# Modulation columns in 1 KB-run half loads, four feature blocks of K in one run, and an earlier load of reciprocal rows, in a transformer-block kernel

## The chip, the cores and the metric

The kernel runs on one core of one Trainium2 chip. The metric is device time in microseconds (us) of that core, from repeated executions; "span" is the same execution as the hardware profiler sees it, about 1.8 us shorter. The granted TensorE clock is given with each run as the mean over its span; 1.0 is full speed.

## The reference

One block of a diffusion transformer: layer norm with modulation, linear attention, and a gated feed-forward, for 2048 tokens of width 1024. The change touches the modulation and the K projection of the first part (cut to what matters):

```python
mod = (_silu(c) @ w_mod).reshape(c.shape[0], 6, 1, -1)
sa, ca, ga, sb, cb, gb = ...                    # shift, scale, gate of either part
h = _layernorm(x, axis=-1) * (1 + ca) + sa      # (2048, 1024)
q, k, v = split(h @ wqkv)                       # 32 heads of 32
pq, pk = phi(q), phi(k)                         # phi(t) = where(t > 0, t + 1, exp(t)) + 1e-6
# ... attention, x = x + ga * o @ wo, then the feed-forward with sb, cb, gb
```

K of any token therefore needs the shift and scale columns of w_mod (2 x 1024 x 1024, 4 MB) as well as wk (2 MB) and x, and all of that comes through one DMA queue.

## The kernel before

K is computed as h (transposed, features on partitions) times wk, in eight feature blocks of 128 that are summed in PSUM. Two feature blocks are a "quarter". For each quarter, TensorE makes the shift (t=0) and scale (t=1) of its 256 features as 32 matmuls with one column each, VectorE copies them out of PSUM and scales two blocks of h with them, and TensorE can run these two blocks of K. "Warming" matmuls of zeros keep TensorE in use while nothing else is there for it. The loads, in the order of the queue:

```python
x_dma(0, 1); x_dma(1, 2)                 # 256 KB a chunk of 128 tokens
wmq_dma(0, (1,))                         # w_mod, one quarter's scale: 512 KB in 512 B runs
x_dma(2, 3)
wmq_dma(0, (0,))                         # the same quarter's shift
w_dma(WK, OFF_WK, "wk", 1, 0, D, 0, 2)   # wk feature blocks 0 and 1, 512 KB in 2 KB runs
x_dma(3, 4)
for q in range(1, 4):
    wmq_dma(q)                           # 2 x 512 KB
    for d0, d1 in ((2 * q, 2 * q + 1), (2 * q + 1, 2 * q + 2)):
        w_dma(WK, OFF_WK, "wk", 1, 0, D, d0, d1)   # 256 KB each
# ... wq, more x
```

The opening as each engine's order has it (cut: the part for quarters 2 and 3 follows in the same manner):

```python
t1(0, 5); ln1_bn(1, 1); ln1_fin(1)       # t1: eight transposes of a chunk; ln1_*: layer norm
warm(6, 7)                               # six warming matmuls
mod_cols(0, 4)                           # 32 one-column matmuls of quarter 0
ln1_bn(2, 0); xhat_dve(1, *xh_buf(1)); t1(1, 6); ln1_bn(2, 1); ln1_fin(2)
mod_copy(0, 4); mod1(0, 1, 0, 2)         # VectorE: copy out, scale blocks 0-1 of chunk 0
warm(3, 7)
k_part(0, [0])                           # K, blocks 0-1, tokens 0-127
# ... k_part(0, [1]), k_part(0, [2]), mod_cols(1, ...), ...
```

The other place is 220 us later, ahead of the feed-forward: `rb_load(3, (0,))`, a broadcast load of reciprocal rows for the attention's denominator, stands behind three DMA transposes in the same queue.

## Time and profile before

| what | before |
|---|---|
| time, three first runs | 834.2 us (833.83 to 834.79) |
| span, mean clock | 832.2 us, 1.0 |
| first K matmul starts | 10.85 us |
| first Q matmul starts | 30.69 us |
| feed-forward starts | 234.42 us |
| wait for the up weights at 252 us | 0.59 us |

The profile is that of one execution. The views used are the page (shares of busy time, the span in 40 slices), the timeline of an engine (start, duration, instructions in a row, and in brackets the idle time before them and who ended it), and the table by stretches (busy time of each engine in each stretch, with the granted clock). A load's landing is the start of its DMA issue plus the time from issue to landing that the tile view gives. How to read them is shown in the prediction below, with the lines themselves.

Matmuls overlap, so durations do not show the rate; starts do. At full clock 512-column matmuls start 0.216 us apart, at half the clock 0.427 us.

### The profile page before, as it was taken

What the parts mean: (1) busy time and instruction counts of PE and PEld (TensorE: products, weight loads), DVE (VectorE), ACT (ScalarE), POOL (GpSimd) and SP (SyncE); (2) the same over time, 40 slices, a digit from 0 to 9 for tenths busy, and PEclk for the clock granted to TensorE, in tenths of its full rate; (3) what the DMA queues carried; (4) which work ended last, traced back from release to release, by engine and by line L of the source; (5) the groups of instructions that cost most, each with busy time, mean ns of one, the idle gap of its engine ahead of it and who ended that gap; (6) DMA issues with size and microseconds to landing.
All of it is one profiled execution on the core that took longest, in us unless ns stands there. A gap on an engine that the chain in (4) does not pass through costs nothing.

```text
span 832.2 us, 11518 instructions
## 1 busy us (share of the span) xinstructions
PE 821.7 (99%) x4179; PEld 391.9 (47%) x4253; DVE 509.7 (61%) x920; ACT 321.3 (39%) x542; POOL 36.2 (4%) x90
## 2 busy tenths in 40 slices
PE   8999999999999999999999999999999999999998
PEld 4444446665444444444444444444444444444445
DVE  6799888834776577753555565355556535555522
ACT  2597642323523354410444441044444104444300
POOL 2122200000200000000000000000000000000000
PEclk9999999999999999999999999999999999999999
DMA  9788769358999789170555533065553306555000
GB/s 288 230 182 223 166 136 274 48 121 195 205 254 289 227 244 262 31 173 19 158 153 152 151 102 76 20 163 152 154 146 102 76 20 171 155 152 137 7 20 26
DMA packets 216929, 121.90 MB, mean 146 GB/s; under 512 B 69276, under 2 KB 206756, under 8 KB 215848
## 3 DMA queue, kind: packets, MB, share of 16 engines
q1 hardware_dynamic: 216856, 121.16, 56.1%
q8 instruction: 34, 0.56, 0.3%
q14 instruction: 23, 0.19, 0.1%
q10 hardware_dynamic: 16, 0.00, 0.0%
HBM read 103.03 MB, written 4.47 MB: 129 GB/s over the span
## 4 chain that ended last, share of the span: by engine, by line
PE 92%; SPq 3%; DMA 3%; issue 1%; DVE 1%; ACT 0%; ACTq 0%
PE ps_all L1359 23%; PE ps_all L1334 22%; PE ps_all L1331 21%; PE ps_all L826 7%; PE ps_all L862 7%; PE ps_all L811 5%; PE ps_all L1193 5%; DMA wu<-in_B_w_up_dram 2%; SPq L568 1%; DMA wmq<-in_w_mod_dram 1%; SPq L1172 1%; SPq L573 1%; PE ps_all L844 0%; PE ps_all L1121 0%; SPq L562 0%
## 5 line engine op out<-in xcount | busy, mean ns | idle before, releaser
L1334 PE MATMUL ps_all<-h2T,wu 128*128 128x512 bf16 x896 | 339.6, 379 | 2.3 <-DMA wu<-in_B_w_up_dram 0.4
L1331 PE MATMUL ps_all<-h2T,wg 128*128 128x512 bf16 x860 | 325.9, 379 | 0.0
L1359 PE MATMUL ps_all<-wd,yT 128*128 128x512 bf16 (+3 forms) x934 | 193.1, 366 | 0.9
L1342 ACT ACTIVATE q<-ps_all 128x512 f32<-128x512 f32 x112 | 66.9, 597 | 222.3 <-PE ps_all L1331 217.1
L1359 PEld LDWEIGHTS ps_all<-wd,yT 128*128 128x128 bf16 x952 | 90.1, 98 | 103.7 <-issue 0.2
L1334 PEld LDWEIGHTS ps_all<-h2T,wu 128*128 128x128 bf16 x896 | 87.7, 98 | 106.5 <-DMA wu<-in_B_w_up_dram 0.9
L1331 PEld LDWEIGHTS ps_all<-h2T,wg 128*128 128x128 bf16 x896 | 87.7, 98 | 105.6
L1347 DVE SCALAR_TENSOR_TENSOR ww<-th,guh 128x512 f32<-128x512 f32 x112 | 77.5, 692 | 77.9 <-ACT th L1346 77.9
L1344 DVE SCALAR_TENSOR_TENSOR ww<-q,ps_all 128x512 f32<-128x512 f32 x112 | 76.9, 687 | 74.5 <-ACT guh L1343 74.3
L1346 ACT ACTIVATE th<-ww 128x512 f32<-128x512 f32 x112 | 70.5, 629 | 87.5 <-DVE ww L1344 87.5
L1364 DVE TENSOR_TENSOR ps_all<-ps_all,gbb 128x512 f32<-128x512 f32 (+3 forms) x34 | 22.7, 667 | 94.6 <-PE ps_all L1359 94.6
L1349 DVE TENSOR_TENSOR yT<-ww,ps_all 128x512 bf16<-128x512 f32 x112 | 76.9, 686 | 3.8
L1343 ACT ACTIVATE guh<-ps_all 128x512 f32<-128x512 f32 x112 | 66.3, 592 | 0.0
L862 PE MATMUL ps_all<-h1T,wq 128*128 128x512 bf16 x256 | 56.7, 379 | 0.0
L1193 PE MATMUL ps_all<-w,pq 128*128 128x512 bf16 x252 | 56.3, 379 | 0.2
L811 PE MATMUL ps_all<-wk,h1T 128*128 128x512 bf16 x239 | 55.3, 379 | 1.2 <-DMA wk<-in_A_wqkv_dram 0.5
L800 ACT ACTIVATE eb<-ps_all 128x512 f32<-128x512 f32 x64 | 36.4, 593 | 38.1 <-PE ps_all L811 14.8
L862 PEld LDWEIGHTS ps_all<-h1T,wq 128*128 128x128 bf16 x256 | 25.0, 98 | 29.9
L1193 PEld LDWEIGHTS ps_all<-w,pq 128*128 128x128 bf16 x256 | 24.9, 98 | 30.0 <-ACT w L1123 0.3
L811 PEld LDWEIGHTS ps_all<-wk,h1T 128*128 128x128 bf16 x248 | 23.6, 97 | 28.9 <-DVE h1T L691 2.3
L826 PE MATMUL ps_all<-xall,pk 128*128 128x342 bf16 (+1 forms) x216 | 35.2, 307 | 0.0
L630 ACT ACTIVATE xhd<-xall,nm,rs 128x1024 bf16<-128x1024 bf16 x12 | 14.9, 1240 | 38.2 <-DVE nm L620 31.7
(97 smaller groups left out, 506.6 us busy)
## 6 DMA issues: line engine op xcount, KB each, us to landing
wg<-in_B_w_gate_dram SPq DMA_DIRECT2D x56, 512.0 KB, 3.9
wu<-in_B_w_up_dram SPq DMA_DIRECT2D x56, 512.0 KB, 5.2
rb<-scr_rd SPq DMA_DIRECT2D x32, 256.0 KB, 5.8
wd<-in_B_w_down_dram SPq DMA_DIRECT2D x7, 1024.0 KB, 8.9
wmst<-in_w_mod_dram SPq DMA_DIRECT2D x6, 1024.0 KB, 6.4
wmq<-in_w_mod_dram SPq DMA_DIRECT2D x8, 512.0 KB, 7.5
out_dram<-xall SPq DMA_DIRECT2D x31, 128.0 KB, 1.7
xall<-in_A_x_dram SPq DMA_DIRECT2D x3, 1024.0 KB, 9.1
```

The costliest lines, as they stand in the source:

```text
L811: o = sch.op(T, lambda e, dc=dc: e.matmul(PS(bank), H1[sg][:, ci, dc, :], W_[:, dc, jg * 512:(jg + 1) * 512], start=(dc == 0), stop=(dc == ...
L826: o = sch.op(T, lambda e, c_=c_: e.matmul(PS(bank, 0, n), PK[c_][:, g * P:(g + 1) * P], xrow(c_, o_, o_ + n), start=(c_ == 0), stop=(c_ == ...
L862: o = sch.op(T, lambda e, dc=dc: e.matmul(PS(b), WQ[:, dc, qc * P:(qc + 1) * P], H1[sg][:, :, dc, :], start=(dc == 0), stop=(dc == NDC - 1 ...
L1193: last[half] = sch.op(T, lambda e, g=g, half=half: e.matmul(PS(b0 + half), PQ[sg][:, g, ci * P:(ci + 1) * P], W2[:, g, half * 512:(half + ...
L1331: og = sch.op(T, lambda e, dc=dc: e.matmul(PS(bg), WG[slot][:, dc, e_ * P:(e_ + 1) * P], H2[sg][:, dc, :], start=(dc == 0), stop=(dc == ND ...
L1334: ou = sch.op(T, lambda e, dc=dc: e.matmul(PS(bu), WU[slot][:, dc, e_ * P:(e_ + 1) * P], H2[sg][:, dc, :], start=(dc == 0), stop=(dc == ND ...
L1342: sch.op(A, lambda e: e.activation(Q1[j][:, :], PS(bg), ACTF.Square, scale=math.sqrt(GELU_A)), prd=pr(bg), wr=rq, note=f"q1 {fc}")
L1344: sch.op(V, lambda e: e.scalar_tensor_tensor(WW[j][:, :], Q1[j][:, :], 1.0, PS(bg), op0=ALU.add, op1=ALU.mult), rd=rq, prd=pr(bg), wr=rw, ...
L1346: sch.op(A, lambda e: e.activation(TH[j][:, :], WW[j][:, :], ACTF.Tanh, scale=GELU_C), rd=rw, wr=rt, note=f"th {fc}")
L1347: sch.op(V, lambda e: e.scalar_tensor_tensor(WW[j][:, :], TH[j][:, :], 1.0, GUH[j][:, :], op0=ALU.add, op1=ALU.mult), rd=rt + rg, wr=rw, n ...
L1349: sch.op(V, lambda e: e.tensor_tensor(YT[:, fc, :], WW[j][:, :], PS(bu), ALU.mult), rd=rw, prd=pr(bu), wr=r_yt(fc), note=f"yT {fc}")
L1359: o = sch.op(T, lambda e, b=b, fc=fc, c0=c0, c1=c1, n=n: e.matmul(PS(b, 0, n), YT[:, fc, ci * P:(ci + 1) * P], WDT[fc // 4][:, fc % 4, c0:c1],
```

## The change

The intent: longer runs (1 KB for 512 B) for the first half of the shift and scale columns, so that they load faster; both halves ahead of wk, so that K of tokens 0 to 383 can go through four feature blocks without a stop for the next quarter; and the reciprocal rows earlier, so that the up weights behind them are not late. The core of the diff (cut marked):

```diff
+        def wmh_dma(t):
+            sch.dma(Q, lambda e: e.dma_start(WMST[1 - t][:], wm_v[:, :, t * D:t * D + 512]), wr=r_wm(1 - t), note=f"wmh{t}")
+
         x_dma(0, 1)
         x_dma(1, 2)
-        wmq_dma(0, (1,))
+        wmh_dma(1)
         x_dma(2, 3)
-        wmq_dma(0, (0,))
+        wmh_dma(0)
         w_dma(WK, OFF_WK, "wk", 1, 0, D, 0, 2)
         x_dma(3, 4)
-        for q in range(1, 4):
+        for d0 in (2, 3):
+            w_dma(WK, OFF_WK, "wk", 1, 0, D, d0, d0 + 1)
+        for q in range(2, 4):
             wmq_dma(q)
 ...
-        warm(6, 7)
-        mod_cols(0, 4)
+        warm(3, 7)
+        mod_cols(0, 4, (1,))
+        mod_cols(1, 4, (1,))
         ln1_bn(2, 0)
         xhat_dve(1, *xh_buf(1))
         t1(1, 6)
         ln1_bn(2, 1)
         ln1_fin(2)
+        xhat_dve(2, *xh_buf(2))
+        mod_cols(0, 4, (0,))
+        t1(2, 7)
         mod_copy(0, 4)
         mod1(0, 1, 0, 2)
-        warm(3, 7)
+        mod1(1, 1, 0, 2)
         k_part(0, [0])
 ... (K of blocks 0 to 3 for tokens 0-383, then the last chunk, then quarters 2 and 3)
             if c_ == 4:
                 pq_scale(1, 1, GH[0] + GH[1])
+                rb_load(3, (0,))
             wo_chunk(c_, 2 * (c_ % 4))
 ...
-            if c_ == 6:
-                rb_load(3, (0,))
```

One half (512 of 1024 features of scale, or of shift) is now one load of 1 MB in 1 KB runs.

More of the change, by code (lines that the diff above doesn't have):

```diff
@@ L723, in mod_cols @@
             rng = [(bank * 2048 + (MC0 + q * 4) * 4, bank * 2048 + (MC0 + q * 4 + 4) * 4)]
+            rq0 = [(bank * 2048 + MC0 * 4, bank * 2048 + (MC0 + 4) * 4)]
             for t in ts:
@@ L726, in mod_cols @@
                     col = MC0 + q * 4 + t * 2 + b
+                    c0 = q * 256 + b * P
                     for dc in range(NDC):
-                        o = sch.op(T, lambda e, t=t, b=b, dc=dc, col=col: e.matmul(
-                            PS(bank, col, col + 1), WMQ[q][:, dc, t, b * P:(b + 1) * P], SILUT[:, dc:dc + 1],
+                        ap = WMST[1 - t][:, dc, c0:c0 + P] if q < 2 else WMQ[q][:, dc, t, b * P:(b + 1) * P]
+                        o = sch.op(T, lambda e, ap=ap, dc=dc, col=col, t=t, b=b: e.matmul(
+                            PS(bank, col, col + 1), ap, SILUT[:, dc:dc + 1],
                             start=(q == b == dc == 0 and t == 1), stop=(dc == NDC - 1), skip_group_check=True),
-                            rd=r_wmq(q, t) + r_sm("siluT"), pwr=(rng if dc == 0 else ()), note=f"mod{q}.{t}.{b}.{dc}")
+                            rd=(r_wm(1 - t, dc, dc + 1) if q < 2 else r_wmq(q, t)) + r_sm("siluT"), pwr=((rng + (rq0 if (q, t) == (1, 0) else [])) if dc == 0 else ()), note=f"mod{q}.{t}.{b}.{dc}")
             for t_ in rng:
@@ L933, in bass_adaLN_cond__linear_attn_block__geglu_ffn__prompt_kernel @@
         ln1_fin(2)
+        xhat_dve(2, *xh_buf(2))
+        mod_cols(0, 4, (0,))
+        t1(2, 7)
         mod_copy(0, 4)
         mod1(0, 1, 0, 2)
-        warm(3, 7)
+        mod1(1, 1, 0, 2)
         k_part(0, [0])
-        xhat_dve(2, *xh_buf(2))
-        t1(2, 7)
-        mod1(1, 1, 0, 2)
+        mod_cols(1, 4, (0,))
         ln1_bn(3, 0)
         ln1_bn(3, 1)
+        mod1(2, 1, 0, 2)
+        mod_copy(1, 4)
+        k_part(0, [1])
+        k_part(0, [2])
         ln1_fin(3)
-        k_part(0, [1])
-        mod1(2, 1, 0, 2)
-        mod_cols(1, 4, (0,))
-        k_part(0, [2])
+        mod1(0, 2, 2, 4)
+        k_tiles([2, 3], [(0, 0), (0, 1)])
+        k_tiles([2], [(1, 0), (1, 1)])
         xhat_dve(3, *xh_buf(3))
-        mod_cols(1, 4, (1,))
-        mod_copy(1, 4)
+        mod1(2, 1, 2, 4)
         t1(3, 7)
-        mod1(0, 3, 2, 4)
-        k_tiles([2, 3], [(0, 0), (0, 1), (1, 0), (1, 1)])
-        k_tiles([2], [(2, 0), (2, 1)])
+        k_tiles([3], [(1, 0), (1, 1)])
+        k_tiles([2, 3], [(2, 0), (2, 1)])
         mod1(3, 1, 0, 4)
+        mod_cols(2, 4, (0,))
         k_part(0, [3])
         k31([2, 3])
-        mod_cols(2, 4, (0,))
-        k_tiles([3], [(2, 0)])
         mod_cols(2, 4, (1,))
         mod_copy(2, 4)
-        k_tiles([3], [(2, 1)])
         k_tiles([2, 3], [(3, 0)])
```

## The prediction

> **What bounds the kernel now.** I read the page's shares of busy time first, then the TensorE timeline with the idle time before each group, then the DMA view of the opening and the timeline of the DMA-issuing queue around the one late wait.
>
> ```profile
> span 832.2 us, 11518 instructions
> PE 821.7 (99%) x4179; PEld 391.9 (47%) x4253; DVE 509.7 (61%) x920; ACT 321.3 (39%) x542; POOL 36.2 (4%) x90
> ```
>
> TensorE is busy for 821.7 of 832.2 us, so only some 10 us are left that are not matmul time, about 2 us of them the launch and 2.5 us the last store. Nothing in this change touches the bulk of the matmuls. The question is where TensorE waits, and the timeline of TensorE tells (start, duration, instructions, idle time before them and who ended it):
>
> ```profile
> 8.70 1.19 PE L728 MATMUL ps_all<-siluT,wmq 128*128 128x1 bf16 x32
> ...
> 10.85 1.03 PE L811 MATMUL ps_all<-wk,h1T 128*128 128x512 bf16 x4
> ...
> 16.49 2.32 PE L811 MATMUL ps_all<-wk,h1T 128*128 128x512 bf16 x10 [0.46 <-DMA wk<-in_A_wqkv_dram]
> ...
> 21.01 0.55 PE L728 MATMUL ps_all<-siluT,wmq 128*128 128x1 bf16 x16 [0.53 <-DMA wmq<-in_w_mod_dram]
> ...
> 27.27 2.97 PE L811 MATMUL ps_all<-wk,h1T 128*128 128x512 bf16 x13 [0.23 <-DVE h1T L691]
> 30.07 0.77 PE L897 MATMUL ps_all<-wk,h1T 128*128 128x496 bf16 x10
> 30.69 13.97 PE L862 MATMUL ps_all<-h1T,wq 128*128 128x512 bf16 x64
> ```
>
> K of the first 512 tokens begins at 10.85 us and the first Q matmul starts at 30.69 us. After that TensorE runs without a gap, but for one, to its last matmul at 829.5 us. So the program is **30.69 us of opening plus a fixed stream of 801.5 us**, and the opening is paced by loads: each short wait in it ends with a piece of w_mod, of wk, or a VectorE step that waited for one. The other gap is here:
>
> ```profile
> 251.69 0.38 PE L1331 MATMUL ps_all<-h2T,wg 128*128 128x512 bf16 x1
> 252.49 0.39 PE L1334 MATMUL ps_all<-h2T,wu 128*128 128x512 bf16 x1 [0.42 <-DMA wu<-in_B_w_up_dram]
> ```
>
> These two matmuls start 0.80 us apart where their neighbours start 0.216 us apart: 0.59 us lost to the up weights' third load.
>
> **What the Trainium skill says.** (1) "DMA: Bandwidth & Descriptors", Specifications, gives 512 B and up as enough for line rate; its section "Why small descriptors are slow (HBM only)" charges some 3 bus cycles per packet beside one per 32 B, from which I estimate 19 against 35 cycles for 512 B and 1 KB: 8% less time per byte. The trace already shows more than that. Its rate of transfer over 8.5 to 30 us, in 40 slices:
>
> ```profile
> GB/s 392 383 390 344 314 296 291 291 298 311 345 357 356 315 294 316 277 294 317 346 355 342 326 299 292 295 283 290 314 358 349 321 341 330 324 351 381 337 377 417
> DMA packets 8846, 7.10 MB, mean 330 GB/s; under 512 B 258, under 2 KB 7446, under 8 KB 8844
> ```
>
> The troughs at about 290 are the w_mod quarters (runs of 512 B), the crests the wk rows (2 KB), and the end, wq halves (1 KB) and x, stays at 320 to 417 without those troughs. (2) The same page, "Queues, rings and completion order": descriptors are consumed in ring order on each engine. The tile view agrees: the fourth quarter's two pieces and the last two wk rows land in the order of issue (24.1, 25.8, 26.4 and 27.1 us). So what is queued first delays all behind it. (3) "TensorE: Matmul & The Clock Gate", Part 1: after an idle window of some 3.4 us the array falls back to half its rate. Here the warming matmuls start 0.427 us apart up to 6.9 us and 0.216 us apart from then on; no fall-back shows later.
>
> **Part 1, the loads.** The bytes are the same. Four loads of 512 KB in 512 B runs become two of 1 MB in 1 KB runs, and the second feature quarter moves ahead of wk. From landings (issue plus time to landing in the tile view): x1 lands at 4.2, the second quarter's two pieces at 13.2 and 15.0, the last at 25.8. Between 4.2 and 15.0 lie four w_mod pieces, two x chunks and 512 KB of wk; a 256 KB row block takes 0.67 us (26.44 to 27.13), so 10.8 - 4 x 0.67 = 8.1, or 2.0 us a piece and 4.0 us per MB. For 1 KB runs: wq and x from 27.13 to 35.7 are 8.5 us for 3 MB, of which x's 1 MB takes 4 x 0.67 = 2.7, so 2.9 us per MB. By the rate alone (290 against about 345 GB/s) it is 3.6 against 3.0. The saving is then 0.6 to 1.1 us per MB, **1.2 to 2.2 us** on every landing from wk's third row on: the last wk row comes at about 25.4 instead of 27.1.
>
> **The price** is that K can only begin later, for both halves now stand before the first wk rows. Estimated landings: first half's shift or scale at 7.6, x2 8.3, the other 11.3, wk rows 0 and 1 at 12.65 (before: about 10.7). VectorE needs the column sums (TensorE 0.41 us for 16), the copy 0.16 and a scaling of 0.27 us before the first K: 11.3 + 0.4 + 0.3 + 0.3 = 12.3, so the wk rows decide, and **K starts at about 12.7, 1.85 us later**.
>
> **Part 2, K in one run.** From 12.7 TensorE has to do: 64 full K matmuls x 0.216 = 13.8, the eight of 16 columns 0.3, 80 column matmuls x 0.0255 = 2.0 and one set of eight transposes 0.45, together 16.6 us. Before, from 10.85, it was 16 column matmuls and 8 transposes more, 17.5 us, in 19.84 us: 2.3 us of waits. After, the waits for loads go (at 12.7 plus the work, each later w_mod piece is in place: the third quarter at about 17 to 19 where TensorE arrives at 18.9 and 20.6, the fourth at 22 to 24 where it arrives at 23.5 and 25). What stays are VectorE's three hand-overs of the next feature blocks: at block 2 some 0.1 to 0.2, at block 4 about 0.3 (copy and scaling end 1.15 us after the column matmuls start; those and two K matmuls cover 0.85), at block 6 about 0.4 (as the 27.27 row now). Sum 12.7 + 16.6 + 0.8 = **30.1 us** for the first Q matmul: 0.6 us gained, not the 1.7 that the loads gained. The load wait is exchanged for TensorE's own work. The warming matmuls dropped (nine become three) cost nothing, as they only filled waits.
>
> **Part 3, the reciprocal rows' load (rb) earlier.** The DMA queue before:
>
> ```profile
> 220.28 8.42 SPq L670 DMA_TRANSPOSE h2T<-xh  x3
> 228.79 1.94 SPq L1172 DMA_DIRECT2D rb<-scr_rd  x4
> ...
> 231.90 5.56 SPq L1172 DMA_DIRECT2D rb<-scr_rd  x4
> ...
> 238.58 5.05 SPq L1272 DMA_DIRECT2D wu<-in_B_w_up_dram  x1
> ```
>
> The queue stands behind a transpose that ScalarE feeds at 227.4; meanwhile the DMA engines run at a share of 0.66 in 224 to 228 us (the table by stretches), some 1.4 us idle. Then two rb loads of 1 MB each (a quarter every 1.2 us) lie ahead of the late wu, which lands at 252.4. The order of instructions shows one set of four rb loads moved ahead of the three transposes. It fills the idle 1.4 us, so wu lands at least 1 us earlier against its need, and the 0.59 us go. The three transposes are pushed back by up to 4.7 us; the first then lands at about 230.5 instead of 225.7 and VectorE's scaling of the four chunks ends at about 234.8 instead of 233.5. The feed-forward begins at 234.4, its first block needs the first scaling alone (about 232.9), and VectorE makes one in 0.27 us where TensorE uses one in 0.43: hidden.
>
> **Sum:** 0.6 + 0.6 = 1.2 us, 834.2 - 1.2 = **833.0 us**.
>
> **Rivals.** (a) *The loads set the end*: no VectorE or TensorE limit, Q starts with the last wk row at 25.4 + 3.45 = 28.9, gain 1.8 + 0.6: 831.8. For it: every wait but one named now is a load's. Against it: the sum of work after a start at 12.7. (b) *K starts too late or VectorE stalls it*: landing of the second half at 12 rather than 11.3, or the third x chunk delaying VectorE's in-order line, moves all by 0.7: no gain in the opening, 833.6. (c) *The clock falls back*: between 8 and 12.7 us TensorE has only 48 one-column matmuls and 16 transposes; if that counts as idle, K runs at 0.427 for some 3.4 us: 1.7 us lost, 834.7. The trace before had a like sparse stretch (8.7 to 10.8) but with three warming matmuls. (d) *The rb load delays the transposes into the feed-forward's start*: up to 1 us lost, 834.0.
>
> **Range and chances.** The work sets (a) and (b) as the ends, with three runs before spread over 1 us: 831.9 to 834.2 holds 8 in 10. Two per cent are 16.7 us, more than the whole opening's waits, so faster by that is 0.005, slower 0.01, within 0.985.
>
> **What would show it.** Right: the first K matmul at about 12.7, the first Q at about 30.1, no load named ahead of TensorE between them, VectorE named ahead of K instead; no wait for wu near 251. Wrong: a load still named at the fourth quarter, 0.427 us between K matmuls, or VectorE named at the start of the feed-forward.

## The result

| | before | after |
|---|---|---|
| time, median (range), 6 runs each | 833.95 us (833.53 to 834.79) | 835.88 us (834.01 to 839.03) |
| mean clock | 1.0 in all | 0.998 in two runs, 0.996 in four |
| ratio after / before | | 1.0024, 95% interval 1.0002 to 1.0045 |

A ratio is the mean time of one kernel's runs over that of the other's of the same rounds, so it is not quite the ratio of the medians quoted. The change is slower by a quarter of a per cent, 2.9 us above the 833.0 predicted and outside the predicted range. It also scatters more: 5 us between its runs, where the kernel before has 1.3.

The page of the changed kernel, its shares of busy time and the granted clock in 40 slices of 20.9 us:

```profile
PE 826.2 (99%) x4247; PEld 392.8 (47%) x4247; DVE 509.4 (61%) x922; ACT 321.1 (38%) x542; POOL 36.6 (4%) x90
...
PEclk8999999999999999999999999999999999999999
```

TensorE's busy time reads 4.5 us more than before (826.2 against 821.7), but that tells nothing of the change: the profile of the kernel before holds 4179 matmuls beside 4253 weight loads, so 74 records are missing, and the first experiment below, with the same opening and all 4253, reads 825.7 at full clock. The clock's row has its 8 in the first slice, so all of it is in the opening. The timeline of TensorE there:

```profile
7.75 0.81 PE L885 MATMUL ps_all<-warm 128*128 128x512 bf16 x3
10.36 0.96 PE L736 MATMUL ps_all<-siluT,wmst 128*128 128x1 bf16 x32 [1.80 <-DMA wmst<-in_w_mod_dram]
12.21 1.04 PE L666 MATMUL ps_all<-ident,xh 128*128 128x128 bf16 x8 [0.89 <-DVE xh L630]
14.04 0.59 PE L736 MATMUL ps_all<-siluT,wmst 128*128 128x1 bf16 x16 [0.79 <-DMA wmst<-in_w_mod_dram]
14.49 1.01 PE L666 MATMUL ps_all<-ident,xh 128*128 128x128 bf16 x8
15.48 1.87 PE L819 MATMUL ps_all<-wk,h1T 128*128 128x512 bf16 x4
...
33.36 13.97 PE L870 MATMUL ps_all<-h1T,wq 128*128 128x512 bf16 x64
...
59.49 2.12 PE L819 MATMUL ps_all<-wk,h1T 128*128 128x512 bf16 x9 [0.28 <-DVE h1T L696]
```

TensorE waits 1.80 us for the first half (prediction: landed at 7.6 us; the sums start at 10.36) and 0.79 us for the other (11.3; landed at 13.99). K starts at 15.48 instead of 10.85, and its first four matmuls take 1.87 us where the same four took 1.03 before: half the clock. The table by stretches, one line of it for the kernel before and then the same one for the changed kernel (stretch in us, its length, busy us and instructions of TensorE matmuls, weight loads, VectorE, ScalarE, GpSimd, then granted clock, DMA share, GB/s):

```profile
12.00:13.00 1.00, 1.00 (x10) 0.45 (x7) 1.00 (x2) 0.64 (x1) 0.00 (x0) 1.00 1.21 293
```

```profile
12.00:13.00 1.00, 0.79 (x8) 0.77 (x8) 0.96 (x3) 0.00 (x0) 0.00 (x0) 0.50 1.08 383
```

The clock is 0.50 here. It leaves 1.00 at about 11.1 us and is back at about 17.96 (0.56 in 11 to 12 us, 0.52 in 17 to 18), 6.83 us in all. The DMA moves more (383 against 293 GB/s), but mostly not in 1 KB runs: of the changed kernel's 235 packets in this microsecond 160 are of 2 KB, from x and wk. The rates to compare are those of stretches that one run length nearly fills: 11 to 13 us before (512 B), then 8 to 10 us in the changed kernel (1 KB).

```profile
DMA packets 1158, 0.59 MB, mean 293 GB/s; under 512 B 18, under 2 KB 1156, under 8 KB 1158
```

```profile
DMA packets 717, 0.76 MB, mean 379 GB/s; under 512 B 12, under 2 KB 682, under 8 KB 717
```

So the 1 KB runs do have a higher rate, which makes the late landings the more surprising.

The place at the feed-forward is as intended. The lines of before are 0.80 us apart; the same pair, 17.27 us after the feed-forward's start in both, now is:

```profile
254.82 0.38 PE L1339 MATMUL ps_all<-h2T,wg 128*128 128x512 bf16 x1
255.04 0.38 PE L1342 MATMUL ps_all<-h2T,wu 128*128 128x512 bf16 x1
```

0.22 us, no wait. And the queue there, with the first set of four reciprocal loads now ahead of the transposes, which the prediction showed behind them:

```profile
223.67 2.19 SPq L1181 DMA_DIRECT2D rb<-scr_rd  x4
225.97 9.07 SPq L675 DMA_TRANSPOSE h2T<-xh  x3
```

The span of the two profiled runs thus adds up from few terms. Starts of the first K and Q matmul, of the feed-forward's first up or gate matmul and of its first down matmul, from the timelines:

| us | before | after | change |
|---|---|---|---|
| K starts | 10.85 | 15.48 | +4.63 |
| K to Q | 19.85 | 17.88 | -1.97 |
| Q to the feed-forward | 203.73 | 204.19 | +0.46 |
| feed-forward's start to its first down matmul | 111.53 | 110.93 | -0.60 |
| from there to the end | 486.28 | 486.27 | -0.01 |
| span | 832.23 | 834.76 | +2.53 |

The +0.46 is the wait for VectorE in the last timeline line (its two matmuls start 0.66 us apart instead of 0.22). The rest is the opening and the earlier reciprocal rows.

### The profile page after: what moved, and what is told of

Same layout as the page of the kernel before. It is cut to its first block, busy times and chain, and to the rows that moved or that the text cites. A ratio compares the mean times of both kernels' runs of the same rounds, so it can differ in the third digit from the quotient of the medians.

```text
span 834.8 us, 11579 instructions
## 1 busy us (share of the span) xinstructions
PE 826.2 (99%) x4247; PEld 392.8 (47%) x4247; DVE 509.4 (61%) x922; ACT 321.1 (38%) x542; POOL 36.6 (4%) x90
## 4 chain that ended last, share of the span: by engine, by line
PE 95%; DMA 2%; ACT 1%; DVE 1%; issue 0%; POOL 0%; SPq 0%; ACTq 0%; POOLq 0%
PE ps_all L1367 23%; PE ps_all L1342 23%; PE ps_all L1339 23%; PE ps_all L834 7%; PE ps_all L1202 7%; PE ps_all L870 5%; PE ps_all L819 5%; DMA wmst<-in_w_mod_dram 1%; DMA h1T<-xh 1%; DVE h1T L696 0%; PE ps_all L852 0%; PE ps_all L1130 0%; PE ps_all L736 0%; ACT xh L643 0%; ACT xh L646 0%
## 5 line engine op out<-in xcount | busy, mean ns | idle before, releaser
L1339 PE MATMUL ps_all<-h2T,wg 128*128 128x512 bf16 x896 | 339.6, 379 | 0.0
L819 PE MATMUL ps_all<-wk,h1T 128*128 128x512 bf16 x248 | 57.7, 384 | 0.4 <-DVE h1T L696 0.4
L809 DVE TENSOR_SCALAR eb<-eb 128x512 f32<-128x512 f32 x64 | 25.7, 418 | 6.8 <-ACT eb L808 6.2
```

The costliest lines, as they stand in the source:

```text
L819: o = sch.op(T, lambda e, dc=dc: e.matmul(PS(bank), H1[sg][:, ci, dc, :], W_[:, dc, jg * 512:(jg + 1) * 512], start=(dc == 0), stop=(dc == ...
L1339: og = sch.op(T, lambda e, dc=dc: e.matmul(PS(bg), WG[slot][:, dc, e_ * P:(e_ + 1) * P], H2[sg][:, dc, :], start=(dc == 0), stop=(dc == ND ...
```

## The experiments

Theory at the outset: the earlier reciprocal rows give what was predicted, and two things in the opening take more than that: K starts later than estimated, since the half loads land late, and the clock falls back in the sparse stretch that the change makes. Rivals: the run length or the loads' size is the cause rather than the order; the clock is a by-product that costs nothing, since loads set the pace. Times are medians of five runs (four and six where told), each beside nine or ten runs of the kernel before on the same chip.

### One part alone: the reciprocal rows

```diff
 (kernel before)
+                rb_load(3, (0,))        # at c_ == 4
             wo_chunk(c_, 2 * (c_ % 4))
-            if c_ == 6:
-                rb_load(3, (0,))
```

> The kernel before with the load of rb for the last quarter of the tokens moved ahead, and nothing else. If the up weights' third load waited behind that load (my step for part 3, and the profile of the changed kernel, which names no wait there), the 0.80 us between two matmuls near 251 us becomes 0.22 and the time falls by 0.6 us, to a ratio of 0.9993, clock 1.0 in every run. Rival: the wait went in the changed kernel only because its TensorE came later; then the wait stays and the ratio is 1.0000.

Measured: 833.12 us against 833.56, ratio 0.9994 (0.998 to 1.0007), clock 1.0 in all runs. The pair near 252 us:

```profile
251.91 0.38 PE L1330 MATMUL ps_all<-h2T,wg 128*128 128x512 bf16 x1
252.13 0.38 PE L1333 MATMUL ps_all<-h2T,wu 128*128 128x512 bf16 x1
```

No wait. From the feed-forward's start to its first down matmul it is 110.94 us instead of 111.53, so 0.59 us are gone where 0.59 were predicted. The times agree (0.44 us), though their interval includes no difference.

### One part alone: the opening

```diff
 (changed kernel, the reciprocal rows put back)
-                rb_load(3, (0,))        # at c_ == 4
+            if c_ == 6:
+                rb_load(3, (0,))
```

> The changed kernel with the load of rb put back where it was: the opening alone. Theory: the whole loss is in the opening and is larger than the total shows, for rb gives 0.6 us back; so 0.6 us slower than the changed kernel of the same clock, some 3 us behind the kernel before in a run with two half-rate windows (clock 0.996) and 1 to 1.5 with one (0.998). Rival: rb's earlier load shares the blame (it pushes the transposes back); then this one is nearer to the kernel before.

Measured: 836.11 us against 833.56, ratio 1.0027 (1.0015 to 1.004), clock 0.996 in three runs and 0.998 in two. The whole loss is in the opening. One thing was not as expected: with the rows late again, the wait for the up weights measures only 0.09 us in this profile (111.04 us from the feed-forward's start to its first down matmul), not 0.59. So in this profile there was hardly anything for the third part to win, and the parts do not add up. The late load of the up weights landed 17.53 us after the feed-forward's start, against 18.02 in the kernel before; what brought it forward is not shown, nor whether other executions have it.

### The clock: warming matmuls put back

```diff
 (changed kernel)
-        warm(3, 7)
+        warm(10, 7)
         mod_cols(0, 4, (1,))
         mod_cols(1, 4, (1,))
+        warm(4, 3)
 ...
         t1(1, 6)
+        warm(5, 3)
```

> The changed kernel with TensorE kept busy in its three idle stretches of the opening: ten warming matmuls for three before the column sums, four after the first 32 of them, five after the second transposes. Theory A (the clock's fall-back costs most): granted clock 1.0 in all runs, no spread of 5 us between runs any more, K matmuls 0.216 us apart from the first one, and 1.0 to 2.0 us less than the changed kernel: 833.8 to 834.8 us. Rival B (late landings cost all, the clock little): clock 1.0 but the first Q matmul still at 33 us and the time unchanged. If both: K still starts at about 15.4 us, Q at about 32.

Measured: 834.88 us against 833.56, ratio 1.0013 (1.0 to 1.0025), clock 1.0 in all runs. Two lines of TensorE's timeline:

```profile
15.32 1.02 PE L819 MATMUL ps_all<-wk,h1T 128*128 128x512 bf16 x4 [0.40 <-DVE h1T L696]
...
32.19 13.97 PE L870 MATMUL ps_all<-h1T,wq 128*128 128x512 bf16 x64
```

K starts nearly as late as in the changed kernel (15.32), but at full speed (four matmuls in 1.02 us), and Q follows 16.87 us later instead of 17.88. The runs lie within 1.5 us again. So, by these ratios, about half of the loss was the clock (1.0027 or 1.0024 down to 1.0013; the intervals overlap), and the rest is K's start.

### The run length: the same order in 512 B runs

```diff
 (changed kernel: each half as two loads of 256 features)
-            sch.dma(Q, lambda e: e.dma_start(WMST[1 - t][:], wm_v[:, :, t * D:t * D + 512]), ...)
+            for h in range(2):
+                sch.dma(Q, lambda e, h=h: e.dma_start(WMST[1 - t][:, :, h * 256:h * 256 + 256], wm_v[:, :, t * D + h * 256:t * D + h * 256 + 256]), ...)
```

> The changed kernel with each 1 MB half loaded as two of 512 KB in runs of 512 bytes, in the same order: the length of the runs alone. Theory of the prediction: 1 KB runs are quicker, so here the second half lands 1 us or more later than the 14.0 us of the changed kernel, and the time is some 1 us longer. Rival (the order of the loads, not the runs, made the landings late): the second half lands at 11 to 12 us as it would by the pace of the kernel before, 2.0 us a piece of 512 KB after 4.2 us plus x, and the time is shorter.

Measured: 836.46 us, ratio 1.0034 (1.0021 to 1.0046), clock 0.994 to 0.998. The halves had landed by 9.1 and 12.94 us, earlier than the changed kernel's 10.3 and 13.99, not later: in these two profiles 1 KB runs bring nothing forward. (The second experiment, with the changed kernel's loads, has them by 9.5 and 13.15, so much of the difference is scatter.) Its profile fell back for three windows, with K to Q at 19.63 us, and it is the only one in which the feed-forward's start waited for VectorE (0.31 us), the prediction's rival (d).

### The clock alone: fewer warming matmuls in the kernel before

```diff
 (kernel before)
-        warm(6, 7)
+        warm(3, 7)
         mod_cols(0, 4)
 ...
         mod1(0, 1, 0, 2)
-        warm(3, 7)
         k_part(0, [0])
```

> The kernel before with the changed kernel's number of warming matmuls: three for six before the column sums, none for three ahead of the first K. Theory (the clock falls back because TensorE waits for megabyte loads, from 8 to 15 us): here the column sums and the first K come at 9 and 10.9 us as before, so no idle window is long enough, granted clock 1.0 in all runs and the time within 0.3 us of the kernel before. Rival (the nine against three warming matmuls are the cause): clock 0.998 or 0.996 in some runs and 1 to 2 us more.

Measured: 834.66 us against 833.68, ratio 1.0014 (1.0001 to 1.0026), clock 0.998 in four of five runs. I had expected nothing, and the rival held. TensorE's timeline:

```profile
11.93 1.48 PE L811 MATMUL ps_all<-wk,h1T 128*128 128x512 bf16 x3 [1.05 <-DVE xh L625]
...
57.18 2.12 PE L811 MATMUL ps_all<-wk,h1T 128*128 128x512 bf16 x9 [0.27 <-DVE h1T L691]
```

Three matmuls in 1.48 us is half the clock; it lasts one window of 3.4 us (11.4 to 14.9). And the wait for VectorE near 57 us, which the changed kernel has at 59.49, is here too. It is in none of the full-clock profiles. So dropping six of the nine warming matmuls costs 1 us with everything else in the program as it was. In the profile Q starts 0.66 us later than in the tenth experiment below, whose K starts as late, and the wait at 57 us adds 0.44. But the one run that kept the full clock took 834.53 us, hardly less than the others (834.59 to 835.29), so the times alone do not tie all of the 1 us to the clock.

### Both at full clock: the size and run length of the loads

Three kernels, each with the added warming matmuls of the third experiment: halves in 512 B runs (as above), halves split by feature blocks so that the runs stay 1 KB,

```diff
+            for h in range(0, NDC, 4):
+                sch.dma(Q, lambda e, h=h: e.dma_start(WMST[1 - t][:, h:h + 4, :], wm_v[:, h:h + 4, t * D:t * D + 512]), wr=r_wm(1 - t, h, h + 4), ...)
```

and whole halves with the third x chunk queued ahead of the first:

```diff
-        wmh_dma(1)
         x_dma(2, 3)
+        wmh_dma(1)
```

> The changed kernel with TensorE kept warm, and each half loaded as two loads of 512 KB in runs of 512 bytes: run length and size of a load, without the clock. If 1 KB runs pay at all (the prediction's 1.2 to 2.2 us), this is 1 us or more slower than the warmed kernel with 1 KB runs (834.9), first Q matmul at 33 us or later. Rival: the landings at the head of the queue are not set by the length of the runs; then it is within 0.5 us of it, the first half whole at 9.1 us and the wk rows at 14.8, as in the run with 512-byte runs and cold clock.

> The changed kernel with TensorE kept warm, and each half in 1 KB runs as two loads of 512 KB (four feature blocks each) in place of one of 1 MB. Theory (a 1 MB load at the head of the queue leaves the DMA engines far apart, so it lands long after most of its bytes moved): the first half lands at 8 to 9 us instead of 10.1, wk's first rows at 13 to 14 instead of 15.2, and the time is 1 us less than the warmed kernel's. Rival (size of a load does not matter): landings and time as in the warmed kernel, within 0.3 us.

> The changed kernel with TensorE kept warm and the third x chunk queued ahead of the first half instead of behind it. VectorE then does not sit 3.4 us in front of the second chunk's normalisation. Theory (the first K is bound by the wk rows at 15.2 us, behind 3.25 MB in the queue): K starts at 15.3 us all the same, time within 0.4 us of the warmed kernel. Rival (VectorE's wait for x is what delays K): K starts up to 1 us earlier and the time falls by as much.

All against 833.68 us of before, all at clock 1.0:

| kernel | time, ratio (interval) | later half landed | K starts | K to Q |
|---|---|---|---|---|
| 512 B runs | 834.26, 1.0009 (0.9996 to 1.0021) | 13.07 | 14.63 | 16.87 |
| 1 KB, split | 833.4, 1.0 (0.9987 to 1.0012) | 13.62 | 15.12 | 16.86 |
| x2 first | 833.89, 1.0 (0.9987 to 1.0014) | 11.88 | 14.58 | 16.87 |

With the clock held, these three are level with the kernel before within their intervals. The landings are of one execution each, and that of the split version was its slowest (834.74 us); its other four took 833.24 to 833.64 us, less than any of the five with 512 B runs (834.1 to 834.7) in the same rounds, with loads of the same size. So 1 KB runs may well be worth some 0.7 us here, the difference of the two means; the landings in the table do not show it. K to Q is one constant, 16.87 us: from K's start on, no load is waited for. That step of the change works as planned. In the third kernel the half had landed at 11.88, but TensorE was warming until 13.4 us; that invited the next try.

### Two attempts to start K earlier

The third x chunk first, one warming matmul instead of five after the second transposes; with split halves, and with whole ones:

```diff
         t1(1, 6)
-        warm(5, 3)
+        warm(1, 3)
```

> The changed kernel with three edits at once: the third x chunk is queued ahead of the first half, each half is two loads of four feature blocks in 1 KB runs, and the warming matmuls of the third experiment are there, but one instead of five after the second set of transposes. Theory (with the clock held, what is left of the loss is the start of K): in the eighth experiment the later half had landed at 11.9 us while TensorE was warming until 13.4, so without four of those matmuls the sums start about 0.9 us earlier, K at about 13.8 instead of 14.6 and Q at about 30.8 to 31.0; time 833.2 to 833.5 against 833.6 to 833.9 for the kernel before. Rival (the clock needs those matmuls): full clock is lost for one 3.4 us window, the span's mean clock reads 0.998 and the time is 834.3 to 835.5.

> The changed kernel with the third x chunk queued ahead of the first half and the fewer added warming matmuls of the ninth experiment, but with the halves whole again (1 MB each in 1 KB runs). In all full-clock profiles of the changed opening so far Q started 16.86 or 16.87 us after K, so the time follows from K alone. Theory A (whole loads behind x2 land early, as in the eighth experiment, where rows 0 and 1 of wk came at 13.24 us): K at 13.3 to 13.8, Q at 30.2 to 30.7, time 832.9 to 833.4, ratio 0.9990 to 0.9997. Theory B (that landing was scatter between executions, as the landings of the kernel before's own opening differ by up to 1.1 us from profile to profile): K at 14.2 to 15.0, Q at 31.1 to 31.9, ratio 1.0003 to 1.0012.

Measured: with split halves 834.17 us against 833.68 (six runs, ratio 1.0007, 0.9995 to 1.002), K at 14.39 and Q at 31.25; with whole halves 834.19 against 834.08 (ratio 1.0, 0.9987 to 1.0014), K at 14.59 and Q at 31.46. Clock 1.0 in all. The full clock held with fewer warming matmuls, but K did not start earlier, because the landings had moved: the later half came at 12.89 and 13.10, not at 11.88. What K waited for in the first of the two was the wk rows:

```profile
14.39 1.02 PE L820 MATMUL ps_all<-wk,h1T 128*128 128x512 bf16 x4 [0.53 <-DMA wk<-in_A_wqkv_dram]
```

So the early landing of the eighth experiment looks like scatter between executions (theory B of the last text), though the ratio of 1.0 lies between the ranges of the two theories. No profile of a changed opening has K before 14.39 us. Some executions were earlier: from Q to the end it is 800.94 us in every full-clock profile with the early reciprocal rows, so a run's span less 800.94 and 16.87 estimates its K, and the split version's four faster runs (spans of 831.4 to 831.8 us) come to 13.6 to 14.0.

### The reciprocal rows again

> The kernel of the first experiment once more, to see whether the earlier reciprocal rows alone beat the kernel before. Theory: the wait for the up weights near 252 us was 0.59 us long and is gone, so 0.5 to 0.6 us faster: ratio 0.9993 to 0.9995, all runs at full clock. Rival (the difference seen was scatter between runs): ratio 0.9998 to 1.0005.

Measured, four runs: 833.27 us against 833.68, ratio 0.9996 (0.9982 to 1.0009), 110.93 us from the feed-forward's start to its first down matmul. In two experiments the median is 0.44 and 0.41 us below the kernel before's, and in both profiles the 0.59 us are gone; but neither interval excludes zero. It is the only version that was tried twice, and it was below the kernel before both times; it is the one to keep.

This run's opening is the kernel before's own, untouched, and yet it was otherwise:

```profile
11.85 1.03 PE L811 MATMUL ps_all<-wk,h1T 128*128 128x512 bf16 x4
...
30.41 13.97 PE L862 MATMUL ps_all<-h1T,wq 128*128 128x512 bf16 x64
```

K one us later than in the first profile, Q 0.28 us earlier. The landings scatter from execution to execution, and that is needed to judge the landings of all the others. It also shows what the change gave away: in the kernel before, later waits absorb a late K (K to Q is 19.85, 20.10 and 18.56 us in its profiles at full clock), while in the changed opening K to Q is 16.87 whatever K's start, so each delay of K's start reaches Q in full.

## What the landings say when put side by side

Feature block 3 of wk has the same bytes in front of it (4 MB, itself included) in every kernel here, and block 7 is the last of the opening. Their landings in one profile each:

| opening | block 3 | block 7 |
|---|---|---|
| before's own, four profiles (fifth experiment included) | 16.34, 16.31, 17.43, 17.16 | 27.13, 27.36, 26.85, 26.86 |
| changed, 1 KB whole, three profiles | 17.42, 16.56, 17.26 | 27.00, 26.27, 26.58 |
| changed, 1 KB split | 17.05 | 26.45 |
| changed, 512 B, two profiles | 16.87, 16.50 | 27.30, 26.82 |
| x2 first, 1 KB: whole, whole, split | 15.30, 16.52, 16.32 | 25.81, 26.10, 26.14 |

For block 3 the kernel before has a mean of 16.81 and a scatter of 1.1 us; 1 KB whole loads have a mean of 17.08, and 512 B runs 16.69. In these profiles nothing is gained there. At block 7, 27.05 becomes 26.58 with the four 1 KB profiles of rows two and three: a gain of about 0.5 us, where I had predicted 1.7. Only with x2 first do both come earlier than before's means, by 0.8 and 1.0 us on average, and those openings have 1 KB runs like the others, so it isn't the runs that tell them apart.

The rate did rise. By 17 us the kernel before's opening had moved 4.68 to 4.76 MB in its four profiles, the three whole-1 KB ones 4.84 to 5.02 (the 512 B runs in the same order 4.70 and 4.84). That is 0.18 MB between the means (4.74 and 4.92), an estimate of 0.5 us at the 340 GB/s of that stretch. Summed over the packet records, as many bytes as end with block 3 had been started by 15.25 us on average in the kernel before's four profiles and by 14.57 in the four 1 KB ones of rows two and three, 0.7 us sooner; but block 3 landed 1.56 us after that before, and 2.50 us after it with 1 KB. The step that failed lies there, between the bytes and the landing. A load counts as landed only when all of it is in, and the packet records show its parts further apart. Counted in order of start, x2's 128 packets (the third lot of 2 KB ones) begin between 4.89 and 7.19 us in the first profile of before, and between 6.42 and 10.41 in the changed kernel; with x2 ahead of the half, between 3.64 and 4.88. So behind a 1 KB half, whole or split, the parts of this transfer are spread over 3.1 to 4.0 us in four profiles (2.2 and 2.3 behind 512 B runs), and the landing waits for the last of them. The records do not say which DMA engine a packet went through, so that single engines fall behind is my reading and not shown. The kernel before's order of loads under the changed order of work was not tried; it would tell the two apart.

## Why the prediction was wrong, step by step

**Where the kernel stands** was right: an opening and a fixed stream. From Q's start to the feed-forward it is 203.73 us in every full-clock profile, and from the first down matmul to the end 486.3 in all. The time is decided by Q's start and the two waits, as the text had it. That "only some 10 us are left" beside TensorE's busy time was a misreading of a profile with 74 matmul records missing: the first experiment, with all of them, has 825.7 of 831.9 us, so 6. Nothing else rests on it.

**"K starts at about 12.7, 1.85 us later"** failed: 15.48, 4.63 us later. The mis-sized term is the landing of wk's blocks 0 and 1, "12.65", which measured 15.35 (14.43 to 15.35 in the six profiles that keep the changed order). Some 1.4 us of the 2.7 could have been read off the profile before. In the new order these blocks end 3.25 MB of queue; the kernel before's own landings of 3 MB (13.18) and 3.5 MB (14.96) put that at 14.07. I had instead used rates of 2.9 us per MB from stretches after 27 us, at the head of a queue that just starts. The remaining 1.3 us is of the size of the scatter of block 3 (1.1 us) plus the whole loads' spread; its cause is not shown.

**"The saving is then 0.6 to 1.1 us per MB, 1.2 to 2.2 us on every landing from wk's third row on"** failed: nothing at block 3, 0.5 us at block 7. Its premise, the higher rate of 1 KB runs, held (379 against 293 GB/s in the lines above); the step from rate to landing did not, since the landings lagged 0.9 us further behind the bytes.

**"Sum 12.7 + 16.6 + 0.8"**: the 17.4 us from K to Q was right but for 0.5: it is 16.87 at full clock. No load is waited for in it, as predicted.

**"The warming matmuls dropped (nine become three) cost nothing, as they only filled waits"** failed, and it is the step that turned a level result into a slower one. The mechanism had been named as rival (c), with the right stretch and the right sign, and was left out of the sum. In the changed kernel's profile it cost 17.88 - 16.87 = 1.01 us from K to Q, and 0.46 us more at 59 us, a VectorE wait whose link to the clock was seen but not explained. With the opening alone it was 18.75, and with 512 B runs 19.63. The fifth experiment shows the fewer warming matmuls alone to do it, and the third, restoring such matmuls, undoes it.

**Part 3** was right in size (0.59 us) and in being hidden from the feed-forward's start: 203.73 us again in both kernels with that part alone. It was wrong to add it to the opening's gain: in the one profile of the changed opening without it the wait is 0.09 us.

**Sum.** The predicted Q was 30.1. K's start adds 2.78, the work takes 0.53 off, the clock adds 1.01: 33.36, the measured start. The range failed since it let K's start vary by 0.7 us and gave the clock no width.

## What to carry to other kernels

To estimate a landing after a reordering, count the bytes in front of it and read the kernel's own landing at that many bytes; then ask how far these landings scatter between executions before believing less than a microsecond. Idle-time work that keeps TensorE in use is part of the schedule: a change that makes waits longer needs more of it, not less, and the granted clock by stretches shows it at once. And waits removed in two places need not add.

## What the Trainium skill lacked or had wrong

- "TensorE: Matmul & The Clock Gate", Part 1, gives an idle window of about 3.4 us as what brings half clock. The window's length agrees (the slow stretches last 3.41, 6.83 and 10.24 us), but a wholly idle one is not needed. In the 3.41 us ahead of the fall-back TensorE was busy for 1.61 us in the changed kernel and for 2.30 us in the fifth experiment. The same part does tell of a kernel whose frequent short idles brought the fall-back; what the page lacks is a figure for how much use counts as busy. These runs give no threshold either: a full-clock profile (the tenth experiment) had 1.98 us in 8.85 to 12.26 us, which is one whole window if they follow on every 3.41 us from 5.44 us, where its trace records the change to full clock.
- The same section puts the cost of the ramp at under 1% of a typical span. The fall-backs here cost no more (1 to 2.8 us of 834), but that is the whole effect of such a change. That it varies from run to run, the page says too: clock 0.998 or 0.996 for the same kernel here, 834.0 to 839.0 us.
- "DMA: Bandwidth & Descriptors", "Why small descriptors are slow (HBM only)", leads to an estimate of 8% less time per byte for 1 KB. The traces show more: 379 against 293 GB/s where one run length nearly fills the stretch, 23% less. No page says that landings need not follow: block 3 of wk landed at a mean of 17.08 against 16.81 us.
- The same page's rule in "Bandwidth", to batch DMAs to 1 MiB or more, did not help at the head of a busy queue: with the clock held, whole 1 MB halves were at 834.88 us against 833.56 of before, the same in two loads at 833.4 against 833.68, though not in the same rounds (ratios 1.0013 and 1.0, overlapping intervals). The later half landed at 13.83 and 13.62 us. The page measured loads issued from GpSimd; these are issued from SyncE.
- No page gives the scatter of landings between executions of the same program: 1.1 us at 17 us in four profiles.
